# Two wider pads in an attention and two-MLP kernel: other places modulo 512 bytes for matmul operands, the same instructions

## The chip, the cores and the metric

The kernel runs on one core of one Trainium2 chip. The metric is the device time of one execution in microseconds (us), as the median of several runs; lower is better. The engines are named as the profile names them: PE is TensorE's matmul side and PEld its weight loads, DVE is VectorE, ACT is ScalarE, POOL is GpSimd, SP is SyncE.

## The reference

Three stages follow each other, all in float32:

```python
p_packed = sm_attn(p, k, v)               # 8 batches, 8 heads, 32 packed queries on 576 keys, head size 64
out = sm_attn(q, p_packed, p_packed)      # 576 queries on the 32 packed rows
x = out as 4608 tokens x 512
x = (silu(x @ w_gate) * (x @ w_val)) @ w_out     # 512 -> 1536 -> 512
h = x @ w_in                                     # 512 -> 2048
return (h * cos(h)) @ w_out2                     # 2048 -> 512
```

sm_attn is softmax(q k^T / 8) v with the row maximum taken off first.

## The kernel before, in words

The order of the work is written out by hand: every engine executes its instructions in the order in which the Python code emits them, and the emission interleaves the engines' side work with TensorE's matmuls step by step. Four stretches follow each other; times are those of the profiled execution.

**Attention and the first up projections** (0 to 435 us). For each of the 8 batches the attention of the next batch is worked into the up projection of the present one. The up projection multiplies folded weights `wp` (stationary) with attention rows `a2` (moving, 288 columns a matmul; line 535, in batch 0 line 524 with `wpp` or `wpf` and `af`). The fold itself is line 495.

**The first down projection** (435 to 702 us, function `strassen`, matmul at line 652). Tokens come in five sets; in four of them the moving tile `g` has 512 columns, in the fourth it has 256. Each set is done as seven products in the order 0, 4, 6, 1, 2, 3, 5 (a Strassen-like scheme), 36 matmuls each: three loads of weights `w1` times 2 output halves, 2 row blocks and 3 passes. A pass pairs the high or low part of a split float32 operand with one of the other (`PASSES`). ACT and DVE split the raw loads `hr` into `g` one product ahead (lines 111 and 112), and between products do the remaining weight preparation (`w2_...`).

**The second up projection** (702 to 1064 us, functions `period` and `product`, matmul at line 971, four single ones at line 984). 24 periods of 84 matmuls: seven products of six (two row blocks, three passes) for each of two overlapping pairs of feature blocks. Stationary is `up`, moving `xs`, 384 columns. ACT and DVE evict, form h cos h and store it to HBM through POOL's queue.

**The second down projection** (1058 to 1420 us, function `down_mm`, matmul at line 1056). Six steps of seven products with 48 matmuls each. Stationary is `wd`, moving `g2`, which lies in the same buffers as `xs` and carries that name in the profile; 384 columns.

A stationary operand is always 128 columns of 4 bytes (512 bytes of each partition); each of the matmuls of lines 652, 971 and 1056 starts its operands at a multiple of 512 bytes from the start of the tile's buffer, since a moving block is 2048, 1024 or 1536 bytes long. So within one pool all operands of these three lines have one place modulo 512 bytes.

Two stacks of pools fill a partition of SBUF, one from the bottom (left), one from the top (right, growing down). A pad at the end of the uppermost right pool moves all that lies under it. In the order of opening, the right stack is pool `pad` (`ident`, `zero`, `pt`, `right_pad`, line 104), then `st` (small tiles of attention), `gates` (weights `wg`, later six buffers that hold `w1` of products 4, 6, 1 and 2), and `ups` (`wp`, `a2` and more). Late in the fifth set of the first down projection `pad` and `gates` are closed and the pool `xs` with its `late_pad` (line 902) takes their place at the top. The left stack has the attention tiles, then `da` and `db` (all of `g`, and `w1` of products 0, 3 and 5), then `late` (`up`, `wd`).

Addresses that the program before gives to the operands, modulo 512:

| matmuls | stationary at | moving at | moving minus stationary, mod 512 |
|---|---|---|---|
| L652, products 0, 3, 5 | `w1` in `da`, `db`: 256 | `g`: 256 | 0 |
| L652, products 4, 6, 1, 2 | `w1` in `gates`: 320 | `g`: 256 | 448 (64 below) |
| L971, L984 | `up`: 256 | `xs`: 448 | 192 |
| L1056 | `wd`: 256 | `xs` (`g2`): 448 | 192 |
| L535 | `wp`: 320 | `a2`: 320, 64, 448, 192 | 0, 256, 128, 384 |

Of the kernel before, what the change touches and what calls it, by code (L numbers as in the profile page):

```python
# [10 lines left out]
F32 = mybir.dt.float32  # L11
# [55 lines left out]
def attention_mlp_kernel(ctx: ExitStack, tc: tile.TileContext, qT, kT, vP, pP, wgv, w12, out):  # L67
# [6 lines left out]
    def pool(n, side=None):  # L74
        kw = {"side": side} if side else {}
        return stage[n].enter_context(tc.tile_pool(name=n, bufs=1, reuse_waits="tile", **kw))

    pad = pool("pad", "right")
# [22 lines left out]
    ident = pad.tile([128, 128], F32, name="ident")  # L101
    zero = pad.tile([128, 128], F32, name="zero")
    pt = [pad.tile([128, NPAIR, NP], F32, name=f"pt{i}") for i in range(2)]
    pad.tile([128, 8], F32, name="right_pad")
    half_pi = cst.tile([128, 1], F32, name="half_pi")
    quarter = cst.tile([128, 1], F32, name="quarter")
    warm = cst.tile([128, 1], F32, name="warm")
# [348 lines left out]
    def w2_flush():  # L456
        while w2_dve:
            w2_dve.pop(0)()

    def w2_step():  # L460
        w2_flush()
        if w2_todo:
            w2_dve.append(w2_todo.pop(0)())
# [133 lines left out]
    def load_h(s_, k, t):  # L597
        if s_ < len(SETS):
            t0, N = SETS[s_]
            for fp in range(3):  # L600
                r = raw1[s_, k, t, fp] = hr_tile((k, t), [128, 2, N], "hr")
                f0 = NP1 * k + 2 * fp
                SP.dma_start(out=r, in_=h1[f0:f0 + 2, :, t0 + N * t:t0 + N * t + N].rearrange("f p n -> p f n"))
# [10 lines left out]
    def prep(s_, n, fp):  # L614
        if s_ >= len(SETS):
            return
        N = SETS[s_][1]
        k, t = {0: (0, 0), 4: (1, 0), 6: (1, 1), 1: (1, 1), 3: (0, 1), 2: (0, 0), 5: (1, 0)}[n]
        g = g1[n, fp] = g_first.pop() if g_first else new_g(N)
        split(raw1[s_, k, t, fp], g[:, 0], g[:, 1])  # L620

    def sums1(s_, i):
        todo = {
            1: [((0, 1), (0, 1), (0, 0), fp) for fp in range(3)],
            2: [((1, 1), (1, 1), (0, 1), fp) for fp in range(3)],
            3: [((0, 0), (1, 1), (0, 0), fp) for fp in range(3)],
            4: [((1, 0), (1, 0), (1, 1), 0)],
            5: [((1, 0), (1, 0), (1, 1), fp) for fp in (1, 2)],
        }
        for to, x, y, fp in todo.get(i, ()):  # L630
            to, x, y = (raw1[s_, k, t, fp] for k, t in (to, x, y))
            DVE.tensor_tensor(out=to, in0=x, in1=y, op=ALU.subtract)
# [55 lines left out]
    late = {}  # L688
# [16 lines left out]
    def load_x2(c):  # L705
        for a in range(2):
            for t in range(2):
                xb[a, t] = xt([128, 2, TH], F32, "xb")
                r0 = 2 * TH * c + TH * t
                SP.dma_start(out=xb[a, t], in_=x2d[2 * a:2 * a + 2, :, r0:r0 + TH].rearrange("k p n -> p k n"))  # L710
# [7 lines left out]
    def sums_x2(n):  # L718
        sum_x2(*(("t1", (0, 1), (0, 0)), ("t2", (1, 1), "t1"), ("t3", (1, 1), (0, 1)), ("t4", (1, 0), "t2"))[n])
        if n == 2:  # L720
            del xb[0, 1]

    def new_xs():
        return late["x"].tile([128, 2, 2, TH], F32R, tag="xs", name="xs", bufs=9)

    def split_x2(n, to):
        if to[n] is None:
            to[n] = new_xs()
        split(xb.pop(RIGHT[n]), to[n][:, 0], to[n][:, 1])

    with tc.manual_schedule():
# [142 lines left out]
        def nxt(s_, i):  # L874
            return (s_, ORDER[i + 1]) if i < 6 else (s_ + 1, ORDER[0])

        for s_ in range(len(SETS)):
            end = s_ == len(SETS) - 1
            for i in range(7):
                evict = strassen(s_, i)  # L880
                sums1(s_, i)
                for fp in range(3):
                    prep(*nxt(s_, i), fp)
                if i == 4:
                    load_h(s_ + 1, 0, 0)
                elif i == 5:
                    load_h(s_ + 1, 1, 1)
                    load_h(s_ + 1, 0, 1)
                elif i == 6:
                    load_h(s_ + 1, 1, 0)  # L890
                for _ in range(STEPS_D[s_][i]):
                    w2_step()
                if (s_, i) == (3, 6):
                    w2_flush()
                if end and i == 1:
                    load_x2(0)
                elif end and i == 4:
                    stage["gates"].close()
                    stage["pad"].close()
                    late["x"] = ctx.enter_context(tc.tile_pool(name="xs", bufs=1, side="right", reuse_waits="tile"))  # L900
                    x_now = [new_xs() for _ in range(7)]
                    late["x"].tile([128, 8], F32, name="late_pad")
                    for n in range(3):
                        sums_x2(n)
                elif end and i == 5:
                    sums_x2(3)
                elif end and i == 6:
                    for n in range(7):
                        split_x2(n, x_now)
                evict()  # L910
# [396 lines left out]
```

## Time and profile before

| | |
|---|---|
| median of 3 runs | 1420.67 us (1418.03 to 1423.08) |
| the profiled execution, its own time | 1422.05 us |
| its span, first to last instruction | 1420.3 us |
| mean granted TensorE clock in it | 0.999 of full speed |
| busy: PE, PEld, DVE, ACT, POOL | 99%, 91%, 80%, 58%, 18% |
| matmuls of L652, L971 with L984, L1056 | 1260, 2020, 2016 |

The profiled execution's own time is its span and 1.75 us around it. In the page of the profile, section 5 groups the instructions by line; a matmul's mean duration there runs from its start to its modelled end and overlaps the next one, so the distance from start to start is not that mean. That distance is read from a stretch between two starts: its length divided by the number of matmuls that start in it. In an answer by windows the count in brackets is of all instructions that touch the stretch, so it is larger by one to three than the number that start in it.

### The profile page before, as it was taken

How to read it: one execution, taken by the hardware profiler on the slowest of the kernel's cores; microseconds unless marked ns; L12 is line 12 of the kernel's file. 1: busy time of each engine (PE TensorE's matmuls, PEld its weight loads, DVE VectorE, ACT ScalarE, POOL GpSimd, SP SyncE). 2: the span in 40 equal slices, each digit the busy share in tenths (PEclk: the TensorE clock that was granted, in tenths of full speed). 3: DMA queues.
4: the chain of work that ended last, by engine and by line, in shares of the span. 5: the costliest groups of instructions: out<-in, count | busy, mean ns of one | idle time of the engine just before them, and what ended most of it. 6: DMA issues, size and time to landing. Idle time of an engine off the chain costs nothing.

```text
span 1420.3 us, 25277 instructions
## 1 busy us (share of the span) xinstructions
PE 1400.6 (99%) x9644; PEld 1286.9 (91%) x9644; DVE 1132.3 (80%) x1515; ACT 829.2 (58%) x1226; POOL 258.6 (18%) x424
## 2 busy tenths in 40 slices
PE   8999999999999999999999999999999999999998
PEld 6678888888898888897899999999999999999998
DVE  6779889888857898997768778787778778787785
ACT  5856666656645555553567777686775444444442
POOL 1112222222220111121011111121211202112020
PEclk9999999999999999999999999999999999999999
DMA  8947978786898746556584233242897765747641
GB/s 343 408 164 275 352 273 301 286 320 249 290 365 315 262 153 245 183 198 242 194 343 155 111 147 144 112 149 108 290 382 243 270 203 188 245 134 262 209 130 34
DMA packets 148504, 329.35 MB, mean 232 GB/s; under 512 B 21664, under 2 KB 58016, under 8 KB 146976
## 3 DMA queue, kind: packets, MB, share of 16 engines
q1 hardware_dynamic: 111040, 202.15, 40.7%
q0 software_dynamic: 36480, 123.76, 22.4%
q10 hardware_dynamic: 864, 1.84, 0.4%
q8 instruction: 76, 1.25, 0.4%
q14 instruction: 44, 0.36, 0.1%
HBM read 202.38 MB, written 125.30 MB: 231 GB/s over the span
## 4 chain that ended last, share of the span: by engine, by line
PE 73%; issue 13%; DVE 5%; DMA 4%; POOL 3%; ACT 2%; SPq 0%; POOLq 0%; DVEq 0%; ACTq 0%
PE o L652 16%; PE o L1056 15%; PE pv L535 7%; PE pg L535 7%; PE ac L971 7%; PE pb L1056 4%; PE pd L1056 4%; PE pd L971 3%; POOL h L991 2%; PE wp L495 2%; PE pb L971 2%; PE pv L524 2%; PE pg L524 1%; DMA hr<-h 1%; PE pp L234 1%
## 5 line engine op out<-in xcount | busy, mean ns | idle before, releaser
L652 PE MATMUL o<-g,w 128*128 128x512 f32 (+1 forms) x1260 | 263.6, 371 | 3.5 <-DVE g L112 1.8
L652 PEld LDWEIGHTS o<-g,w 128*128 128x128 f32 x1260 | 218.8, 188 | 47.9 <-DVE g L112 2.8
L1056 PE MATMUL o<-xs,wd 128*128 128x384 f32 x1440 | 254.3, 336 | 0.5 <-DVE xs L112 0.5
L1056 PEld LDWEIGHTS o<-xs,wd 128*128 128x128 f32 x1440 | 251.9, 187 | 0.9 <-DVE xs L112 0.9
L971 PE MATMUL ac<-xs,up 128*128 128x384 f32 x1152 | 219.5, 338 | 0.6 <-ACT v L1008 0.6
L971 PEld LDWEIGHTS ac<-xs,up 128*128 128x128 f32 x1152 | 204.5, 187 | 1.0 <-ACT v L1008 0.9
L112 DVE TENSOR_TENSOR xs<-raw,xs 128x768 fp32r<-128x768 f32 x168 | 149.6, 950 | 36.1 <-ACT xs L111 36.1
L111 ACT ACTIVATE xs<-raw 128x768 fp32r<-128x768 f32 x168 | 132.4, 843 | 73.1 <-DVE raw L1095 70.8
L111 ACT ACTIVATE g<-hr 128x1024 fp32r<-128x1024 f32 (+1 forms) x105 | 101.1, 975 | 91.8 <-PE o L652 42.3
L535 PE MATMUL pv<-a,wp 128*128 128x288 f32 x1008 | 150.6, 298 | 2.9 <-DVE h L567 2.8
L535 PEld LDWEIGHTS pg<-a,wp 128*128 128x128 f32 x1008 | 137.7, 188 | 16.8 <-issue 5.7
L535 PE MATMUL pg<-a,wp 128*128 128x288 f32 x1008 | 150.3, 298 | 0.5 <-ACT E L208 0.5
L535 PEld LDWEIGHTS pv<-a,wp 128*128 128x128 f32 x1008 | 137.6, 188 | 11.5 <-DVE h L567 5.7
L112 DVE TENSOR_TENSOR g<-hr,g 128x1024 fp32r<-128x1024 f32 (+1 forms) x105 | 113.1, 1113 | 35.5 <-ACT g L111 35.2
L553 ACT ACTIVATE silu<-pg 128x576 f32<-128x576 f32 x96 | 62.4, 651 | 112.8 <-PE pg L535 103.9
L971 PE MATMUL pd<-xs,up 128*128 128x384 f32 x576 | 117.2, 338 | 0.0
L567 DVE TENSOR_TENSOR h<-silu,pv 128x576 f32<-128x576 f32 x96 | 72.1, 751 | 52.2 <-PE pv L535 17.2
L971 PEld LDWEIGHTS pd<-xs,up 128*128 128x128 f32 x576 | 102.8, 187 | 0.0
L568 POOL DMA_DIRECT2D h<-h x96 | 53.4, 556 | 243.6 <-DVE h L567 221.7
L1105 POOL DMA_DIRECT2D out<-ot x80 | 49.5, 622 | 243.7 <-DVE ot L1100 181.5
L1095 DVE TENSOR_TENSOR raw<-raw,raw 128x768 f32<-128x768 f32 x96 | 85.3, 948 | 3.0 <-DMA raw<-h 3.0
L1011 DVE TENSOR_TENSOR hs<-v,pd 128x384 f32<-128x384 f32 x96 | 53.0, 552 | 33.7 <-PE pd L971 29.7
(130 smaller groups left out, 2065.6 us busy)
## 6 DMA issues: line engine op xcount, KB each, us to landing
raw<-h SPq DMA_DIRECT2D x96, 384.0 KB, 7.6
wd<-w2d SPq DMA_DIRECT2D x136, 256.0 KB, 4.0
h<-h POOLq DMA_DIRECT2D x96, 288.0 KB, 5.4
hr<-h SPq DMA_DIRECT2D x48, 512.0 KB, 7.5
raw<-in_w SPq DMA_DIRECT2D x44, 512.0 KB, 5.0
h<-cp POOLq DMA_DIRECT2D x48, 384.0 KB, 2.9
h<-cs POOLq DMA_DIRECT2D x48, 384.0 KB, 2.8
up<-w2u SPq DMA_DIRECT2D x56, 256.0 KB, 6.4
```

Source lines behind the costliest of these rows:

```text
L111: ACT.activation(out=hi, in_=src, func=AF.Copy)
L112: eng.tensor_tensor(out=lo, in0=src, in1=hi.bitcast(F32), op=ALU.subtract)
L535: PE.matmul(out=p_[:, c, :HS], lhsT=w[:, u, x, o:o + 128], rhs=a2[b][:, u, y, HS * c:HS * c + HS], start=(n == 0), stop=(n == 5),)
L553: ACT.activation(out=s_, in_=pg[:, :, :HS], func=AF.Silu)
L567: DVE.tensor_tensor(out=h_, in0=s_, in1=pv[:, :, :HS], op=ALU.mult)
L568: nc.gpsimd.dma_start(out=h1[f, :, S * b:S * b + S], in_=h_.rearrange("p c n -> p (c n)"))
L652: PE.matmul(out=acc[:, m, :N], lhsT=wd1[n, fp][:, j, 256 * x + 128 * m:256 * x + 128 * m + 128], rhs=g1[n, fp][:, y, j, :], start=(first a ...
L971: PE.matmul(out=out, lhsT=w[:, u, 128 * k:128 * k + 128], rhs=x[:, v, k, :], start=(first and k == 0 and i == 0), stop=(k == 1 and i == 2) ...
L1011: DVE.tensor_tensor(out=out, in0=x, in1=y, op=ALU.add)
L1056: PE.matmul(out=acc[m], lhsT=wd[n, 2 * fp + j][:, x, 128 * m:128 * m + 128], rhs=g2[n, fp][:, y, j, :], start=(first and fp + j + q == 0), ...
L1095: DVE.tensor_tensor(out=to, in0=x, in1=y, op=ALU.subtract)
L1105: eng.dma_start(out=out[r0:r0 + TH, c0:c0 + 64].rearrange("(b r) d -> r b d", r=32), in_=ot[32 * al:32 * al + 32].rearrange("p b m c -> p ...
```

## The change

Two pads, which nothing reads or writes, become wider. `right_pad` goes from 8 to 24 float32 (32 to 96 bytes of each partition): all pools on the right that are open with it, `st`, `gates` and `ups` among them, and the tiles of `pad` itself lie 64 bytes lower. `late_pad` goes from 8 to 56 (32 to 224 bytes): the nine `xs` buffers lie 192 bytes lower. Nothing on the left moves, and no instruction is added, removed or put in another place.

```diff
     pt = [pad.tile([128, NPAIR, NP], F32, name=f"pt{i}") for i in range(2)]
-    pad.tile([128, 8], F32, name="right_pad")
+    pad.tile([128, 24], F32, name="right_pad")
     half_pi = cst.tile([128, 1], F32, name="half_pi")
...
                     x_now = [new_xs() for _ in range(7)]
-                    late["x"].tile([128, 8], F32, name="late_pad")
+                    late["x"].tile([128, 56], F32, name="late_pad")
                     for n in range(3):
```

With it `w1` in `gates` is at 256, `xs` at 256, and all of L652, L971, L984 and L1056 have stationary and moving operand at 256. In L535 both operands move by 64, so the differences stay.

## Rows read from the trace of the kernel before

**Rows 1.** The page: busy time by engine, and the granted clock in 40 slices.

```profile
PE 1400.6 (99%) x9644; PEld 1286.9 (91%) x9644; DVE 1132.3 (80%) x1515; ACT 829.2 (58%) x1226; POOL 258.6 (18%) x424
...
PEclk9999999999999999999999999999999999999999
```

**Rows 2.** Waits of PE from 420 us on: us in total, times, longest.

```profile
PE o L652 <- DVE g L112: 1.8, 3, 0.8
PE o L652 <- ACT g L111: 1.7, 1, 1.7
PE ac L971 <- ACT v L1008: 0.6, 1, 0.6
PE o L1056 <- DVE xs L112: 0.5, 1, 0.5
PE pb L1056 <- DVE xs L112: 0.2, 1, 0.2
```

**Rows 3.** Windows, L652, 512 columns: products 4, 6, 1, 2, then 3, 5, 0, alternating.

```profile
443.75:477.35 33.60, 33.60 (x146) 27.07 (x144) 1.00 0.73 269
477.35:501.86 24.51, 24.51 (x110) 20.27 (x109) 1.00 0.86 308
501.86:535.45 33.59, 33.59 (x145) 27.07 (x144) 1.00 0.38 136
535.45:559.96 24.51, 24.51 (x109) 20.27 (x108) 1.00 0.89 332
559.96:593.56 33.60, 33.60 (x145) 27.07 (x144) 1.00 0.33 115
```

**Rows 4.** Windows, L652, 256 columns: products 4, 6, then 3, 5.

```profile
614.22:618.46 4.24, 4.24 (x38) 4.24 (x37) 1.00 0.26 102
618.46:622.72 4.26, 4.26 (x38) 4.20 (x37) 1.00 0.05 22
632.08:636.40 4.32, 4.32 (x38) 4.32 (x37) 1.00 1.01 369
636.40:640.72 4.32, 4.32 (x38) 4.32 (x37) 1.00 1.03 349
```

**Rows 5.** Windows, all engines: 20 periods of L971; L1056's third, fourth, and 32 later products.

```profile
core 0: us, PE busy (x) PEld busy (x) DVE busy (x) ACT busy (x) POOL busy (x), PEclk, DMA share, GB/s
747.85:1044.65 296.80, 296.80 (x1682) 296.80 (x1681) 229.31 (x292) 220.08 (x355) 57.43 (x80) 1.00 0.44 165
1077.15:1085.63 8.48, 8.48 (x49) 8.48 (x49) 5.91 (x8) 2.50 (x3) 0.00 (x0) 1.00 0.89 307
1086.96:1094.76 7.80, 7.80 (x47) 7.80 (x46) 7.80 (x12) 2.81 (x4) 1.26 (x2) 1.00 0.50 180
1137.15:1405.44 268.29, 268.29 (x1537) 268.29 (x1537) 211.75 (x273) 115.16 (x164) 39.60 (x64) 1.00 0.55 181
```

**Rows 6.** Windows, all engines: where DVE is densest.

```profile
490.00:600.00 110.00, 110.00 (x479) 89.53 (x478) 99.43 (x111) 60.79 (x76) 14.91 (x25) 1.00 0.56 202
600.00:702.00 102.00, 98.52 (x547) 84.70 (x546) 86.00 (x112) 52.74 (x78) 15.07 (x26) 1.00 0.56 200
```

**Rows 7.** Timeline of PE: start, us, operation, count, idle before it and its releaser.

```profile
623.78 25.29 PE L652 MATMUL o<-g,w 128*128 128x256 f32 x179 [0.67 <-DVE g L112]
650.74 0.50 PE L652 MATMUL o<-g,w 128*128 128x512 f32 x1 [1.67 <-ACT g L111]
652.00 8.67 PE L652 MATMUL o<-g,w 128*128 128x512 f32 x36 [0.76 <-DVE g L112]
661.05 41.59 PE L652 MATMUL o<-g,w 128*128 128x512 f32 x179 [0.39 <-DVE g L112]
```

**Rows 8.** Timeline of PE: the last L535 matmuls, 12 to a run, and what follows.

```profile
430.79 1.76 PE L535 MATMUL pv<-a,wp 128*128 128x288 f32 x12
432.39 1.76 PE L535 MATMUL pg<-a,wp 128*128 128x288 f32 x12
433.98 1.75 PE L535 MATMUL pv<-a,wp 128*128 128x288 f32 x12
435.57 4.71 PE L652 MATMUL o<-g,w 128*128 128x512 f32 x20
```

**Rows 9.** Groups by line and form, PE: busy us, mean ns of one.

```profile
L535 PE MATMUL pv<-a,wp 128*128 128x288 f32 x1008 | 150.6, 298 | 2.9 <-DVE h L567 2.8
L495 PE MATMUL wp<-wg,ppT 64*32 64x512 f32 x752 | 46.5, 596 | 1.1 <-DVE wg L139 1.1
L524 PE MATMUL pv<-af,wpp 128*128 128x288 f32 x80 | 21.4, 411 | 0.0
L267 PE MATMUL s<-qt,ppT 64*32 64x288 f32 x256 | 9.9, 409 | 0.5 <-ACT ppT L257 0.5
```

## The prediction

> **What bounds the kernel now.** I read the page first, then PE's waits, then windows cut exactly at the starts of products, then DVE's share where it is densest. The page says that TensorE is busy for 99% of the span, at its full granted clock in every slice [rows 1]. PE's waits from 420 us on add up to 4.8 us [rows 2]; the other engines have time left, most of all in the last two stretches (DVE 229 of 297 us and 212 of 268 us [rows 5]). So the span is the sum of the distances from one matmul's start to the next, and a change that touches only addresses can act only through these distances. The question is whether they depend on where the operands lie.
>
> The windows say that something like it does. The reader should divide each length by the matmuls that start in it. In the first down projection a set's products 4, 6, 1 and 2 are 144 matmuls of 512 columns and take 33.60 us, **233.3 ns** each; products 3, 5 and the next set's 0 are 108 and take 24.51 us, **226.9 ns** each; this alternates set by set to the hundredth of a microsecond [rows 3]. Shape, line, passes and moving buffers are the same, and PE does not wait. What separates the two kinds is the weights' pool: in the first the stationary operand lies 64 bytes above the moving one modulo 512, in the second at the same place. The pool is confounded with the place, but nothing else in the code is. At 256 columns the order is turned round: 117.8 and 118.3 ns at 64 apart (4.24 and 4.26 us for 36), 120.0 ns at the same place (4.32 us) [rows 4]. So the same place is not always the cheaper one; the price depends on the width too.
>
> **The change part by part.** No instruction, wait or transfer is added, removed or moved in any queue; what changes is the distance of matmuls in three stretches.
>
> *First down projection, 512 columns.* Four sets of four products of 36 matmuls, 576 in all, go to the configuration that products 0, 3 and 5 already have, stationary 256 and moving 256, so the price is a measured one: 233.3 - 226.9 = 6.4 ns, times 576 is 3.7 us. Not all of it counts. In the last set PE waits for ACT and DVE three times, 1.67, 0.76 and 0.39 us [rows 7]; between the second and the third wait lies one product of 36, and what it gains (0.23 us) becomes wait. The bounds of this term are 3.5 us, and about 1 us if all that is gained ahead of the waits at 623 and 650 us is spent there. I take 3.5: before them DVE is busy for 99 of 110 us, and for 86 of 102 us in the stretch that holds them [rows 6], so DVE follows PE up to there and starts earlier by as much.
>
> *First down projection, 256 columns.* 144 matmuls go from about 118.1 to 120.0 ns: a loss of 0.3 us, perhaps hidden in the waits that follow [rows 7]. I count it. The line's sum is 3.2 us.
>
> *Second up projection.* 384 columns have no row at the same place. The nearest rows are the same place at 256 and 512 columns, 120.0 and 226.9 ns [rows 3, 4]; halfway is 173.5 ns. The halfway rule can be tried on the other configuration: at 64 apart the rows give 118.1 and 233.3, halfway 175.7; the 384-column rows, 192 apart, are 296.80 us / 1680 = 176.7 ns and 268.29 / 1536 = 174.7 ns [rows 5], whose mean is 175.7. The distances there differ (192 above, not 64 below), so that is support, not proof. I take 173.5: 176.7 - 173.5 = 3.2 ns, times 2020 matmuls (L971 and L984) is 6.5 us. The waits of this line are one of 0.6 us [rows 2], and DVE and ACT have a quarter of their time free, which covers a period that is 0.27 us shorter.
>
> *Second down projection.* The same shape and places, but two distances: 176.7 ns (8.48 us for 48) before the stall at 1086 us, 174.7 in the later products [rows 5]. In the product right after that stall 45 matmuls take 7.80 us, 173.3 ns, again with the same places. So the spacing can change at unchanged addresses, after a stall. To 173.5 the gain is 1.2 ns times 1872, 2.2 us, and 3.2 times 144, 0.5 us. I drop the second part, since DVE is busy through the whole stretch of that stall (7.80 of 7.80 us [rows 5]) and the three products ahead of it would only wait longer. The term is 2.2 us.
>
> The bounds for these 4032 matmuls: below, the excess over columns divided by 2.4 GHz (the granted level) that the far 256-column rows show, 118.1 - 106.7 = 11.4 ns, gives 171.4 ns and a gain of 17 us; above, the excess of the far 512-column rows, 233.3 - 213.3 = 20.0 ns, gives 180.0 ns and a loss of 17 us. I take the value between the two same-place rows because their own excesses, 13.3 and 13.6 ns, agree with each other within 0.3 ns and the far ones do not.
>
> *The rest.* L535 moves both operands by 64 bytes, so their difference stays; a run of 12 takes 1.59 to 1.60 us now, 133 ns each [rows 8]. I take nothing. Were the absolute place to matter by as much as in the 256-column rows, 1.9 ns, 2016 matmuls would give or take 4 us. L495 moves both operands too; L524 and L267 change their difference, but already run at several differences within one group, and their groups hold 21 and 10 us [rows 9]: nothing, within 0.5 us.
>
> **Sum**: 3.2 + 6.5 + 2.2 = 11.9 us off. The profiled execution took 1422.05 us, 1.75 of it around its span of 1420.3; its own sum is 1410.2. The median of the runs, 1420.67, lies 1.4 us below it, and the forecast against that is **1408.8 us**.
>
> **A rule against it.** The 512-column rows show two spacings for one shape [rows 3]. The Trainium skill, "SBUF — State Buffer", section "Who interferes with whom", says that PE has two independent read ports, one for the moving operand and one for the weights, and that PE never waits on anyone. By that rule the relative place of the two would be free, and the change would do nothing. The row speaks against it, unless the pool and not the place makes the 6.4 ns; that case is the second rival.
>
> **The rivals.**
> 1. *The late matmuls gain nothing.* The spacing of 384 columns is set by how the stream of matmuls falls into step after a stall, as the stretch at 1086 us suggests [rows 5], not by the distance. Then only line 652 gains its 3.2 us: 1417.5 us. For it: three spacings at one placement. Against it: the 512-column rows keep to theirs in every set [rows 3]. Chance 0.12.
> 2. *Placement does nothing at all*, the two kinds of line 652 differ for another reason that goes with the pool, and the time stays 1420.7 us. Against it: both kinds read tiles of one size by one line, and DVE and ACT do the same for both. Chance 0.04.
> 3. *The same place is the worse one at 384 columns*, as it is at 256 [rows 4]. Place: lines 971 and 1056. Price: up to 180.0 ns, so 3.3 ns times 2020 and 5.3 times 2016, 17.4 us lost, less the 3.2 of line 652: 1434.9 us. It decides once the late matmuls' mean rises by over 3.2 us / 4036 = 0.8 ns, from 175.7 to 176.5; it is seen as a slowdown from 0.3% when the rise is 1.9 ns. Against it: the 512-column rows prefer the same place, and 384 lies between. Chance 0.08.
> 4. *The late matmuls fall to 171.4 ns or under*, the lower bound: 17 us plus 3.2 off, 1400.1 us. Chance 0.06.
>
> **How the numbers follow.** The forecast, that the same place costs columns / 2.4 plus some 13.5 ns at every width, has 0.70. A measurement of this kernel can tell about 0.3%, 4.3 us, from no change. Faster by more than that are the forecast and rival 4, 0.76; within it are rivals 1 and 2, 0.16; slower is rival 3, 0.08. The forecast's own spread is 4 us for L535 and 2 for the waits and the scatter of the runs, 1404 to 1413. The range reaches up to rival 1, to 1418, and down to 1404; left out are rivals 2, 3 and 4 with 0.18.
>
> **What would show it.** In the trace after, all seven products of a 512-column set in the first down projection should take 8.16 us, where four took 8.40; the 256-column ones 4.32 each; a period of the second up projection 14.57 us instead of 14.84, and a product of the second down projection 8.33 instead of 8.38. L535 runs of 12 should still take 1.60 us. PE's waits from 420 us on should stay at 5 to 6 us. The prediction is wrong if the products of line 652 stay unequal (rival 2), if they become equal while a late period stays at 14.8 us (rival 1) or rises (rival 3), or if waits of PE for ACT or DVE grow by what the matmuls gain.

## The result, and the profile after

The changed kernel takes **1409.53 us** (median of 4 runs, 1408.2 to 1412.68) against 1421.0 us before on the same chip (4 runs, 1418.03 to 1423.08): a ratio of 0.9916, 95% interval 0.9895 to 0.9938. The forecast was 1408.8 us and faster.

The profiled execution took 1412.68 us, with a span of 1410.9 us. The windows below are cut like those of [rows 3], at the starts of products: L652 at 512 columns, products 4, 6, 1, 2, then 3, 5, 0, alternating. The columns are the stretch, its length, PE and PEld busy with the instructions that touch it, the granted clock, the share of the DMA engines and GB/s.

```profile
443.81:476.45 32.64, 32.64 (x145) 27.03 (x144) 1.00 0.75 276
476.45:500.93 24.48, 24.48 (x109) 20.27 (x108) 1.00 0.88 310
...
```

All seven products now cost 8.16 us: 32.64 / 144 and 24.48 / 108 are both 226.7 ns. The difference between the two kinds of [rows 3] is gone. At 256 columns (the answer to [rows 4]: products 4 and 3) both kinds are at 120.0 ns, the dearer of the two values before:

```profile
611.33:615.65 4.32, 4.32 (x39) 4.32 (x38) 1.00 0.25 101
629.49:633.81 4.32, 4.32 (x38) 4.32 (x37) 1.00 0.98 358
```

The same three kinds of stretch as in [rows 5], without the one after the stall: 20 periods of L971, L1056's third product, 32 later ones (here with DVE, ACT and POOL too):

```profile
744.41:1035.74 291.33, 291.33 (x1682) 291.12 (x1682) 227.85 (x292) 219.18 (x355) 57.30 (x80) 1.00 0.44 167
1067.63:1075.95 8.32, 8.32 (x49) 8.19 (x49) 4.96 (x7) 0.88 (x2) 0.00 (x0) 1.00 0.86 259
1129.91:1396.14 266.23, 266.23 (x1537) 266.23 (x1537) 211.74 (x273) 115.30 (x164) 39.51 (x64) 1.00 0.55 182
```

They are 291.33 / 1680 = 173.4 ns, 8.32 / 48 = 173.3 ns and 266.23 / 1536 = 173.3 ns, where before there were 176.7, 176.7 and 174.7. DVE's and ACT's busy times are those of before, to within 1.7 us. PE's waits from 420 us on:

```profile
PE o L1056 <- DVE xs L112: 2.1, 1, 2.1
PE o L652 <- ACT g L111: 1.7, 1, 1.7
PE o L652 <- DVE g L112: 1.4, 2, 0.8
PE ac L971 <- ACT v L1008: 0.6, 1, 0.6
```

They sum to 5.8 us against 4.8 [rows 2]; the one that grew is the wait in L1056's fourth product. From the timeline the stretches of this execution can be set against those of before:

```profile
435.63 1.55 PE L652 MATMUL o<-g,w 128*128 128x512 f32 x6
...
699.85 1.23 PE L971 MATMUL ac<-xs,up 128*128 128x384 f32 x6
...
1048.91 2.24 PE L1056 MATMUL o<-xs,wd 128*128 128x384 f32 x12
```

Before, these three starts were at 435.57 [rows 8], 702.48 and 1058.07 us. The first down projection took 264.2 us against 266.9, the second up projection up to L1056's first matmul 349.1 against 355.6, and the rest to the end of the span 362.0 against 362.2. The last two microseconds that were forecast for that rest are missing in this execution. Part of them went into the second of two stretches at half clock, which the next windows show:

```profile
core 0: us, PE busy (x), PEclk, DMA share, GB/s
646.50:649.28 2.78, 0.50 (x1) 1.00 1.05 415
649.28:652.68 3.40, 3.21 (x8) 0.50 1.05 393
...
1077.00:1079.36 2.36, 0.90 (x5) 1.00 1.05 400
1079.36:1082.76 3.40, 3.40 (x13) 0.50 0.37 142
```

Twice the granted clock fell to half, 1.2 instead of 2.4 GHz, for 3.4 us. The first fall came in the second of two waits of PE, 1.73 and 0.76 us with one matmul between them; the second came 0.9 us after a wait of 2.09 us. Work of 1.7 us takes 3.4 us at half the clock, so each cost at most 1.7 us. The change alone does not bring them. The kernel before had waits of 1.67 and 0.76 us at the first place [rows 7] and kept its clock [rows 6]; profiled again (below), it has such a fall behind a wait of 1.86 us in its last stretch. In a second profile of the changed kernel (below) PE waits the same 2.09 us at the second place and the clock stays up, while the 1.73 us at the first place are 0.16. The span of that profile is 1407.6 us, 3.3 us shorter, and not by the clock alone: the first down projection is 3.1 us shorter there (by the shorter wait and without the fall) and the last stretch 1.0, while the part before 436 us is 0.8 us longer.

### The profile page after: what moved, and what is told of

It reads as the page before. It is cut to its first block, busy times and chain, and to the rows that moved or that the text cites. A ratio compares the mean times of both kernels' runs of the same rounds, so it can differ in the third digit from the quotient of the medians.

```text
span 1410.9 us, 25277 instructions
## 1 busy us (share of the span) xinstructions
PE 1389.9 (99%) x9644; PEld 1279.8 (91%) x9644; DVE 1130.3 (80%) x1515; ACT 828.4 (59%) x1226; POOL 258.0 (18%) x424
## 4 chain that ended last, share of the span: by engine, by line
PE 74%; issue 13%; DVE 5%; POOL 3%; DMA 3%; ACT 2%; SPq 0%; POOLq 0%; DVEq 0%; ACTq 0%
PE o L652 17%; PE o L1056 16%; PE pv L535 7%; PE pg L535 7%; PE ac L971 7%; PE pb L1056 4%; PE pd L1056 4%; PE pd L971 3%; PE wp L495 3%; POOL h L991 3%; PE pb L971 2%; PE pv L524 2%; PE pg L524 1%; DMA hr<-h 1%; PE pp L234 1%
## 5 line engine op out<-in xcount | busy, mean ns | idle before, releaser
L652 PE MATMUL o<-g,w 128*128 128x512 f32 (+1 forms) x1260 | 261.3, 370 | 3.1 <-ACT g L111 1.7
L652 PEld LDWEIGHTS o<-g,w 128*128 128x128 f32 x1260 | 220.4, 189 | 43.7 <-ACT g L111 2.2
L1056 PE MATMUL o<-xs,wd 128*128 128x384 f32 x1440 | 253.8, 336 | 2.1 <-DVE xs L112 2.1
L1056 PEld LDWEIGHTS o<-xs,wd 128*128 128x128 f32 x1440 | 251.3, 189 | 2.5 <-DVE xs L112 2.3
L971 PE MATMUL ac<-xs,up 128*128 128x384 f32 x1152 | 215.7, 334 | 0.6 <-ACT v L1008 0.6
L971 PEld LDWEIGHTS ac<-xs,up 128*128 128x128 f32 x1152 | 201.1, 188 | 1.0 <-ACT v L1008 0.9
L535 PE MATMUL pv<-a,wp 128*128 128x288 f32 x1008 | 150.6, 298 | 2.9 <-DVE h L567 2.7
L535 PEld LDWEIGHTS pg<-a,wp 128*128 128x128 f32 x1008 | 137.7, 188 | 16.8 <-issue 5.7
L535 PE MATMUL pg<-a,wp 128*128 128x288 f32 x1008 | 150.3, 298 | 0.4 <-ACT E L208 0.4
L535 PEld LDWEIGHTS pv<-a,wp 128*128 128x128 f32 x1008 | 137.6, 188 | 11.4 <-DVE h L567 5.7
L971 PE MATMUL pd<-xs,up 128*128 128x384 f32 x576 | 115.4, 334 | 0.0
L971 PEld LDWEIGHTS pd<-xs,up 128*128 128x128 f32 x576 | 101.0, 188 | 0.2
L997 DVE SCALAR_TENSOR_TENSOR cp<-ac,cp 128x768 f32<-128x768 f32 x48 | 45.9, 955 | 40.4 <-ACT cp L994 39.7
```

The lines of the kernel that those rows point to most:

```text
L535: PE.matmul(out=p_[:, c, :HS], lhsT=w[:, u, x, o:o + 128], rhs=a2[b][:, u, y, HS * c:HS * c + HS], start=(n == 0), stop=(n == 5),)
L652: PE.matmul(out=acc[:, m, :N], lhsT=wd1[n, fp][:, j, 256 * x + 128 * m:256 * x + 128 * m + 128], rhs=g1[n, fp][:, y, j, :], start=(first a ...
L971: PE.matmul(out=out, lhsT=w[:, u, 128 * k:128 * k + 128], rhs=x[:, v, k, :], start=(first and k == 0 and i == 0), stop=(k == 1 and i == 2) ...
L997: DVE.scalar_tensor_tensor(out=out, in0=h_, scalar=1.0 / TWO_PI, in1=out.bitcast(I32), op0=ALU.mult, op1=ALU.subtract)
L1056: PE.matmul(out=acc[m], lhsT=wd[n, 2 * fp + j][:, x, 128 * m:128 * m + 128], rhs=g2[n, fp][:, y, j, :], start=(first and fp + j + q == 0), ...
```

## Experiments

Spacings below are worked out as above: four products of L652 (144 matmuls), 20 periods of L971 (1680), 32 products of L1056 (1536), from windows of PE alone whose columns are stretch, length, PE busy, clock, DMA share and GB/s.

**One pad at a time: right_only.**

```diff
-    pad.tile([128, 8], F32, name="right_pad")
+    pad.tile([128, 24], F32, name="right_pad")
```

> Only right_pad is widened (24 floats); late_pad stays at 8, so xs stays 192 bytes above its weights modulo 512. If the relative place of the two operands sets the spacing (theory A): all seven products of a 512-column set in L652 take 8.16 us, the 256-column ones 4.32 us, while L971 keeps 14.84 us a period and L1056 8.38 to 8.48 us a product; about 3 us off the time before, 1418. If the late lines gain by following an earlier start rather than by their own addresses (rival B), their periods would shorten here too, and the time would fall by more than 6 us. If nothing depends on the place (rival C): 1421.

```profile
501.32:533.96 32.64, 32.64 (x146) 1.00 0.38 138
742.84:1039.64 296.80, 296.80 (x1681) 1.00 0.44 165
1133.75:1405.11 271.36, 271.36 (x1537) 1.00 0.55 179
```

L652 has its 226.7 ns, L971 keeps 176.7, so rivals B and C are out: these two lines follow their own operands. L1056 did not keep its 174.7 ns: with xs where the kernel before has it, it ran at 271.36 / 1536 = 176.7 ns throughout. The median is 1413.08 us (10 runs, 1410.64 to 1421.81), a ratio of 0.9983, 0.9964 to 1.0002; the interval reaches no change, so it is the trace and not the time that speaks here. The kernel before ran at 1416.6 us on this chip (19 runs, 1414.31 to 1420.31): the medians are 3.5 us apart, near the 3 us expected, though at 1413 and not at 1418. The profiled execution, 1421.81 us, is the longest of the ten.

**late_only.**

```diff
-                    late["x"].tile([128, 8], F32, name="late_pad")
+                    late["x"].tile([128, 56], F32, name="late_pad")
```

> Only late_pad is widened (56 floats); right_pad stays at 8. Theory A: L652 keeps 33.60 us for its four unequal products, L971 falls to 14.56 us a period and L1056 to 8.32 us a product; 6.5 + 2.7 = 9 us off, less what waits take back: 1412 to 1413. The two parts then add up to the whole change. Rival B: L971 and L1056 keep 14.84 and 8.38 us.

```profile
502.56:536.16 33.60, 33.60 (x145) 1.00 0.37 136
746.29:1037.58 291.29, 291.29 (x1681) 1.00 0.44 167
1131.82:1398.06 266.24, 266.24 (x1537) 1.00 0.55 182
```

The mirror image: 233.3 ns in L652's four products, 173.4 and 173.3 ns in the late lines. 1414.16 us (10 runs, 1412.37 to 1416.9), ratio 0.9982, 0.9972 to 0.9992. In the spacings of L652 and L971 the two parts add up. In the medians they don't: late_pad alone lands near the 1412 to 1413 us that were expected, but that is 2.4 us under the 1416.6 us of the kernel before on this chip, and not 9, since the kernel before ran 4.4 us under its first median. Counted from the equal placement on the same chip (1408.99 us, the next run), unequal places cost 5.2 us in L652 alone (this run), 4.1 us in the late lines alone (right_only) and 7.6 us in both.

**Another place, the same difference: all_at_320.**

```diff
-    pad.tile([128, 8], F32, name="right_pad")
+    cst.tile([128, 16], F32, name="left_pad"); pad.tile([128, 8], F32, name="right_pad")
...
-                    late["x"].tile([128, 8], F32, name="late_pad")
+                    late["x"].tile([128, 40], F32, name="late_pad")
```

> A pad of 16 floats on the left moves up, wd, g and w1 of products 0, 3, 5 to 320; right_pad stays at 8 (w1 in gates at 320) and late_pad is 40 (xs at 320). Every pair of L652, L971 and L1056 is again at one place, but that place is 320 and not 256. Theory A (only the difference counts): the same as the changed kernel, 226.7 ns, 120.0 ns, 173.3 ns, 1409 to 1412 us. Rival D (256 itself is a good place, as a multiple of 256 bytes): spacings of 173.3 and 226.7 are lost, 1417 us or more.

```profile
501.87:534.51 32.64, 32.64 (x146) 1.00 0.39 138
742.52:1033.84 291.32, 291.32 (x1681) 1.00 0.46 166
1126.23:1392.47 266.24, 266.24 (x1538) 1.00 0.59 182
```

1408.99 us (4 runs, 1407.84 to 1409.29), ratio 0.9941, 0.9921 to 0.9961, with the spacings of the changed kernel. The place itself does not matter, the difference does; rival D is out.

**256 bytes apart: dist_256.** right_pad 88 and late_pad 120 floats.

> right_pad 88 and late_pad 120 floats: the moving operands of L652 (products 4, 6, 1, 2), L971 and L1056 lie 256 bytes from the stationary ones modulo 512. If the period of the effect is 512 bytes, as the change's words say, spacings differ from those at the same place: more than 174 ns at 384 columns, other than 226.7 at 512. If the period is 256 bytes or less (rival E), all spacings are those of the changed kernel: 226.7, 120.0 and 173.3 ns. L535 gives a hint of E: its differences 0 and 256 have medians of 131 ns alike, 128 and 384 have 133.

```profile
501.32:533.96 32.64, 32.64 (x146) 1.00 0.37 138
741.77:1033.05 291.28, 291.28 (x1681) 1.00 0.44 167
1126.18:1392.42 266.24, 266.24 (x1538) 1.00 0.55 182
```

As at the same place in all three, 1408.95 us (one run). Rival E holds: what counts is the difference modulo 256 bytes, or a divisor of it; "modulo 512" says more than is needed.

**The kernel before again: before_again.** No edit.

> The kernel before, unchanged, looked at a second time. If the spacing at 192 apart depends on how the stream falls into step (theory F, drawn from 174.7 us in one trace of L1056 and 176.7 in the run with right_pad alone at the same places), the far lines' spacings differ between this trace and the first: 171 to 177 ns in L971 or L1056, while products 0, 3 and 5 of L652 repeat 226.7 to 227.1 ns. If the place alone fixes the spacing, L971 repeats 176.7 and L1056 174.7.

```profile
502.36:535.96 33.60, 33.60 (x146) 1.00 0.37 136
535.96:560.46 24.50, 24.50 (x109) 1.00 0.90 332
746.83:1043.63 296.80, 296.80 (x1682) 1.00 0.44 165
1138.59:1406.87 268.28, 268.28 (x1537) 1.00 0.55 181
```

Every spacing repeats, L1056's 174.7 too. So this trace alone did not support theory F; the run with right_pad alone, at the same places, still did. The execution took 1423.46 us, another one on the same chip 1419.74.

**128 bytes apart: dist_128.** right_pad 56, late_pad 24.

> right_pad 56, late_pad 24: 128 bytes between the operands. If the period of the effect is 128 bytes, everything is as at the same place: 226.7, 120.0, 173.3 ns. If it is 256 bytes (theory A, corrected), the spacings are others; L535 at 128 and 384 has medians of 133 and 134 against 131, which asks for 1.5 to 3 ns more at 384 columns, 175 to 176.5 ns, and a time of 1414 to 1417 us.

```profile
501.71:535.18 33.47, 33.47 (x145) 1.00 0.37 135
...
745.62:1041.31 295.69, 295.69 (x1682) 1.00 0.44 165
1135.59:1405.92 270.33, 270.33 (x1537) 1.00 0.55 180
```

232.4 ns, 176.0 ns and 176.0 ns: dearer, so the period is 256 bytes and not 128. The one time, 1422.61 us, is 5 us over what I had expected, but the spacings account for it: over those of the changed kernel they cost 5.7 ns times 576, 2.6 times 2020 and 2.7 times 2016, 14 us, and 14 over its second profile's 1409.38 is 1423.4. It is the expected time that was mis-sized.

**64 bytes above: dist_64.** right_pad 40, late_pad 40.

> right_pad 40, late_pad 40: the moving operand 64 bytes above the stationary one, where the kernel before has it 192 above (64 below, modulo 256). If the sign of the difference does not matter, the spacings are those of before: 233.3 ns at 512 columns, 117 to 118 at 256, 174.7 to 176.7 at 384. If a moving operand ahead of the weights is another case than one behind, they differ by over 1 ns from both kinds seen so far.

```profile
501.72:534.68 32.96, 32.96 (x146) 1.00 0.37 137
612.75:616.83 4.08, 4.08 (x38) 1.00 0.27 107
626.54:630.78 4.24, 4.24 (x39) 1.00 0.89 294
...
745.90:1037.15 291.25, 291.25 (x1681) 1.00 0.44 167
1131.43:1397.67 266.24, 266.24 (x1538) 1.00 0.56 182
```

The sign matters. With the moving operand 64 bytes above the stationary one, 384 columns cost 173.4 and 173.3 ns, as cheap as at the same place, where 64 below (192 modulo 256) cost up to 176.7. 512 columns cost 228.9 ns, between 226.7 and 233.3; product 4 of 256 columns takes 4.08 us, 113.3 ns, the cheapest seen, but product 2, behind a wait of PE, takes 4.24 us, 117.8 ns. One run took 1414.23 us, with two falls of the clock to half for 3.4 us each in its trace.

**32 bytes above: dist_32.** right_pad 32, late_pad 48.

> right_pad 32, late_pad 48: the moving operand 32 bytes above the stationary one. If the effect counts in blocks of 64 bytes, 32 apart is the same block as 0 apart for half of the reads and the spacings are within 1 ns of 226.7 and 173.3; if it is graded in bytes, they lie between those of 0 and of 64.

```profile
502.07:535.66 33.59, 33.59 (x145) 1.00 0.37 135
...
745.75:818.55 72.80, 72.80 (x422) 1.00 0.37 137
833.24:1041.00 207.76, 207.76 (x1177) 1.00 0.46 175
1133.18:1399.42 266.24, 266.24 (x1538) 1.00 0.55 182
```

Neither expectation. 512 columns cost 233.3 ns, more than at 0 or 64, so there is no gradation in bytes. And one placement has two spacings within one line of one execution: of the 20 periods of L971 the first five (420 matmuls) cost 173.3 ns a matmul and the last fourteen (1176) 176.7. The step comes at 826.5 us, behind a single distance of 185 ns between two starts, and PE has no wait in the whole stretch. L1056 then begins at 176.7 ns and costs 173.3 after the wait in its fourth product. The one time is 1415.95 us.

The changed kernel has such single longer distances in L971 too, one of 185 ns at 825.7 us, and goes back to its spacing behind each. The period that holds this one and the period after it, 84 matmuls each, in the first profile of the changed kernel:

```profile
817.23:831.82 14.59, 14.59 (x85) 1.00 0.48 182
831.82:846.38 14.56, 14.56 (x85) 1.00 0.27 109
```

**The changed kernel again: after_again.** No edit to it.

> The changed kernel once more, timed in more rounds beside the kernel before. Theory A with theory F (spacings at one place are steady, those at 192 apart depend on how the stream falls into step): the changed kernel stays within 1408 to 1411 us, the kernel before scatters more widely, 1414 to 1423; the ratio is between 0.990 and 0.996. If the spread of before came from something that both kernels share, both would scatter alike.

```profile
501.72:534.36 32.64, 32.64 (x145) 1.00 0.39 138
742.13:1033.39 291.26, 291.26 (x1681) 1.00 0.44 167
1126.59:1392.83 266.24, 266.24 (x1537) 1.00 0.56 182
```

1409.49 us (6 runs, 1408.15 to 1411.78), ratio 0.9933, 0.9913 to 0.9954. The kernel before beside it: 1418.87 us (11 runs, 1415.24 to 1428.04). The kernels do not scatter alike, as theory F said, though both went over their expected bounds, 1411 and 1423 us. The changed kernel's ten runs over two occasions lie within 4.5 us, the 37 of before over five occasions within 14.

**The first up projection: first_up_64 and first_up_32.** A pad of 16 (or 8) floats between `wp` and `a2`, on top of the change:

```diff
-            wp0.append(ups.tile([128, 2, 2, 512], F32, tag="a2", name="wpp", bufs=2))
+            ups.tile([128, 16], F32, name="mid_pad"); wp0.append(ups.tile([128, 2, 2, 512], F32, tag="a2", name="wpp", bufs=2))
```

> The changed kernel with a pad of 16 floats between wp and a2 in the pool ups: L535's differences, 0 and 128 modulo 256 before, become 64 and 192. A matmul of 288 columns costs 131.5 and 133 to 134.5 ns now. If the rule of the other widths holds (64 above costs as little as or less than 0, 192 costs more), the sum over both halves stays within 1 ns a matmul, 2 us; if 288 columns behave as 256 do (115.6 at 64, 117 at 192, 120 at 0), it falls by up to 3 ns on 2016 matmuls: 6 us, 1403 us, a version that beats both kernels. All other lines as in the changed kernel.

> The same with a pad of 8 floats: L535's differences are 32 and 160 modulo 256. At 32 apart 256 columns cost 117.1 ns and 512 cost 233.5: for 288 columns I expect something between first_up_64 and the changed kernel, 130 to 134 ns. If 288 columns do not react to the place at all, as 131.5 against 133 ns at 0 and 128 might also come from which half it is, the spacings stay 131.5 and 133 to 134.5.

Runs of 12 matmuls of L535 in first_up_64, then in first_up_32 (timeline: start, length, operation, count):

```profile
431.68 1.75 PE L535 MATMUL pv<-a,wp 128*128 128x288 f32 x12
433.27 1.75 PE L535 MATMUL pg<-a,wp 128*128 128x288 f32 x12
```

```profile
431.49 1.76 PE L535 MATMUL pg<-a,wp 128*128 128x288 f32 x12
433.09 1.76 PE L535 MATMUL pv<-a,wp 128*128 128x288 f32 x12
```

A run takes 1.59 us and 1.60 us, as before [rows 8]. first_up_64 gives 1409.18 us (4 runs, 1407.78 to 1412.01), ratio 0.9933, 0.991 to 0.9957: the changed kernel's time; first_up_32 took 1410.81 us in one run. The hoped-for 6 us are not there. The place does count here too, but what one half gains the other loses: the distances within the two halves of a run are 131.7 and 134.1 ns on average in the changed kernel's second profile, 132.6 and 132.6 in first_up_64, 134.0 and 132.8 in first_up_32 (halves in which no distance is over 160 ns). Since 288 columns are 1152 bytes, the two column halves of this line always lie 128 bytes apart modulo 256, and no single pad serves both.

**The unequal placements moved by 256: dist_192_448.** right_pad 72, late_pad 72.

> right_pad 72, late_pad 72: the two unequal placements of the kernel before with their difference moved by 256 bytes, L652 from 448 to 192 and the late lines from 192 to 448. If the period is 256 bytes (what dist_256 showed for the same place), both keep the spacings of before: 233.3 to 233.5 ns at 512 columns, 116 to 118 at 256, 176.7 in L971, 174.7 or 176.7 in L1056. If 256 was only good by itself, they differ by more than 1 ns. A value of L1056 other than the two seen would be a third step of the stream at one placement.

```profile
502.71:536.31 33.60, 33.60 (x145) 1.00 0.38 135
...
746.86:1043.66 296.80, 296.80 (x1681) 1.00 0.44 164
1136.93:1403.17 266.24, 266.24 (x1537) 1.00 0.55 182
```

233.3 ns and 176.7 ns, as before: the period of 256 bytes holds for an unequal placement too. L1056 now shows the third step: 173.3 ns over all 32 products, at a placement (192 modulo 256) that gave it 174.7 in two traces and 176.7 in one. In all four its second and third product, ahead of the wait in the fourth, cost 176.7. The one time is 1419.69 us.

## Why the prediction was right

- *PE's spacings are the span.* Right. With the instructions the same, right_pad alone cheapened only L652 and late_pad alone only L971 and L1056.
- *L652, 512 columns: 6.4 ns on 576 matmuls.* Measured 6.7 ns (8.40 to 8.16 us a product): the forecast's 226.9 was a mean over the three products that follow the dear ones, and in the changed kernel they cost 226.7 as well. At 256 columns it is 120.0 ns, as forecast. The stretch gained 2.7 us in the profiled execution, with up to 1.7 us lost to the half clock within it; without that 4.4, against 3.2 in the sum. Between the second profiles of both kernels, where no fall disturbs this stretch, it gained 4.2 us, 0.65 of them by a shorter wait for ACT (0.81 and 0.16 us). The wait at 661 us, for which the sum took off 0.23 us, is in none of the three later profiles of the two kernels, so taking that off was too strict.
- *384 columns: halfway between the same-place rows, 173.5 ns.* Measured 173.3 to 173.4 in every trace with equal placement, modulo 256. The second up projection gained 6.5 us between the profiles, the sum's own figure. The halfway rule worked here; it does not work everywhere: at 32 bytes 256 and 512 columns cost 117 and 233.3 ns, halfway 175, and 384 columns cost 173.3 or 176.7.
- *Second down projection: 2.2 us.* The spacing is right (32 products gained 2.1 us), the stretch of the profiled execution gained only 0.2. The fourth product waited 2.09 us instead of 0.54 for a split that waits for loads of `h`, and then the clock fell. The 0.54 was the exception: from L1056's first matmul to the end of that wait it is 28.4 us in the first profile of before, but 29.8 in its second, and 29.6 and 29.7 in the two of the changed kernel. Cheaper products ahead of that wait did not bring its end forward, so the 0.5 us that the sum dropped there was rightly dropped.
- *Rival 1, a spacing set by how the stream falls into step.* Not the outcome, but half true: at unequal placement L1056 had 173.3, 174.7 and 176.7 ns in different executions, and L971 two of these in one (32 bytes). At equal placement there was one value in every trace. So the change removes a scatter as well as a cost. That this is why the kernel before scatters fits but is argued, since only profiled executions have a trace. An estimate from right_only supports it: its profiled execution took 1421.81 us; with L1056 at 173.3 ns (3.3 ns times 2016, 6.7 us) and without its waits of 1.7 and 0.5 us it would take 1412.9, and its two lowest runs took 1410.64 and 1410.72. So in those L971 can hardly have cost 176.7 ns throughout either, as it did in every trace at 192 bytes.
- *Rival 2 and the rule behind it.* Out: the spacing of one shape moved with an address alone. The Trainium skill, "SBUF — State Buffer", section "Who interferes with whom", has PE's two read ports independent and PE waiting on nobody. The measurement decides: 226.7 against 233.3 ns a matmul by the place of one operand. What in the chip couples the two streams no run here shows.
- *Rival 3, dearer at the same place.* True at 256 columns only, 120.0 ns against 113.3 at 64 above and 117.8 at 192 (product 4). The bounds speak of 4032 late matmuls where there are 2020 + 2016 = 4036; nothing hangs on it.

The medians, 1421.0 to 1409.5, are 11.5 us apart, against 11.9 in the sum. The direction and the spacings were foreseen; that the size fits this well is partly luck. The sum took the prices of the late lines from one execution of the kernel before, and at unequal placement they differ from execution to execution. On a later occasion the same two kernels were 9.4 us apart (1418.87 and 1409.49 us), and on another chip equal places at 320 were worth 7.6 us (1416.6 and 1408.99). The profiled spans differ by 9.4 us. What held each time is the level of the kernel with equal places, 1409 to 1409.5 us.

## What to carry to other kernels

When PE never waits and one line of matmuls still has two spacings, compare the addresses of its operands: here the place of the moving operand against the stationary one, modulo 256 bytes, is worth up to 6.7 ns of 227. Equal places were cheapest at 512 columns and as cheap as any at 384, and above all gave one spacing where others gave several, so measure before tuning further; only at 256 columns was another place cheaper. Where a spacing can take several values, one trace prices it for that execution alone: compare the times of many runs before counting the gain. A pad costs a few bytes, but pair it with the layout: a block length that is no multiple of 256 bytes brings its own offsets that a pad can't undo.

## What the runs showed of the hardware that was not expected

Places modulo 256 bytes, moving minus stationary, and the spacings of all traces in ns:

| difference | 512 columns | 256 columns, product 4 | 384, L971 | 384, L1056, later products |
|---|---|---|---|---|
| 0 | 226.7 | 120.0 | 173.4 | 173.3 |
| 32 | 233.3 | 117 | 173.3, then 176.7 | 173.3 |
| 64 | 228.9 | 113.3 | 173.4 | 173.3 |
| 128 | 232.4 | 119 | 176.0 | 176.0 |
| 192 | 233.3 | 118 | 176.7 | 173.3, 174.7 or 176.7 |

At 2.4 GHz the values at 0 are 544, 288 and 416 cycles: columns plus 32, at all three widths. At unequal placement a spacing can hold for hundreds of microseconds and then be another: in the next execution (L1056 at 192), behind a wait of PE (L1056 at 32 from 176.7 to 173.3 ns, 256 columns at 64 from 113.3 to 117.8), or behind a single longer distance between two matmuls with no wait at all (L971 at 32). And behind a wait of 2.09 us at one place the clock fell to half for 3.4 us in one execution of the changed kernel and stayed up in another, with no difference in the program.
